# phi of the memory layers without a relu: exponential on ScalarE, clamp on GpSimd, maximum on VectorE

## The chip, the cores and the metric

The kernel runs on one core of one Trainium2 chip. The metric is the device time of one execution in microseconds (us), as the median of a few runs; lower is better. The names of the engines in the profile: PE is TensorE's matmul, PEld its weight load, ACT is ScalarE, DVE is VectorE, POOL is GpSimd, SP is SyncE, which only issues DMAs here.

## The reference

Four layers follow each other, A, B, A, B, each with a layer norm ahead of it and a residual addition behind it. The input x is 2048 x 640; there are 32 heads of 20 columns. The change concerns layer B, which splits the 2048 rows into four segments of 512:

```
phi = lambda t: jnp.where(t > 0, t + 1.0, jnp.exp(t))
for s in range(N):
    qs, ks, vs = q[:, :, s], k[:, :, s], v[:, :, s]
    logits = jnp.einsum("bhqd,bhkd->bhqk", qs, ks) * scale + mask
    p = _softmax(logits, axis=-1)
    a_dot = jnp.einsum("bhqk,bhkd->bhqd", p, vs)
    pq = phi(qs)
    num = jnp.einsum("bhld,bhde->bhle", pq, M)
    den = jnp.einsum("bhld,bhd->bhl", pq, z)[..., None] + 1e-6
    a_mem = num / den
    outs.append(g * a_mem + (1.0 - g) * a_dot)
    pk = phi(ks)
    M = M + jnp.einsum("bhld,bhle->bhde", pk, vs)
    z = z + jnp.einsum("bhld->bhd", pk)
```

So phi(q) is multiplied by a memory M that sums phi(k) v over the earlier segments, and the product is divided by phi(q) times the sum z of phi(k). A common factor of all phi(q), or of all phi(k), drops out of num / den, apart from the 1e-6. Layer A is linear attention with a similar phi, which the change leaves as it is.

## The kernel before

**Numbers.** The float32 weights are scaled by a power of two and split into an upper and a lower float16 part (`w_prep`). Two columns of 128 equal values come with each weight: `inv`, which brings a product of the scaled weight back to its true size, and `scl`, its reciprocal. A projection is three float16 matmuls per block of rows, summed in a PSUM bank in float32 (`proj_t`, L414, 128x512; `proj_n`, L429, 128x320).

**Layer B, one segment** (`b_project`): first v by `proj_n`; then, for five tiles of 128 columns, q and k by `proj_t`, in turns, each into one PSUM bank p of 128x512. `split_store` reads p twice (ScalarE L860, VectorE L861) and writes q or k in two float16 parts to DRAM, from where the attention loads them (`stacks`, L1031). Then `phi` reads p: on ScalarE an exponential with the factor `inv` (L453) and a relu with the same factor (L455); VectorE forms min(e, 1) + r (L456). phi of q is made for segments 1 to 3, phi of k for segments 0 to 2: 2 layers x 3 segments x 5 tiles x 2 = 60 calls. phi of k is turned by TensorE (L888) and multiplied with v into the memory (L898); phi of q meets the memory in `read_mem` (L482), which also divides (L489 to L492).

**Softmax attention** runs beside the projections and the layers' other work, by heads of four: scores of queries for the row maxima (`row_max`, L1045; VectorE takes the maximum with the mask, L1051), scores of keys with the maxima taken off (L1086), an exponential per bank on ScalarE (L1090), the causal cut of the diagonal block on GpSimd (L1097), and the product with v (`weigh`, L1113).

**Order.** Two generators, the layers' dense work and the attention, are woven by an estimated cost of TensorE; that order is fixed for TensorE (`MANUAL`). On the other engines a scheduler sets the order by what is ready in its model. The eight PSUM banks come from one pool (`bank`), and the allocator picks for each new tile a bank that its model sees free; TensorE's first matmul into it waits until the last reader of the tile before is done. The SBUF tiles of phi come from a pool named "er" with three buffers, which `phi_a` of layer A and `normalize` also use.

The functions and lines that the change touches: `w_prep` (the clamp L266), `scales` (L319 to L321), `phi` (L449 to L456), `read_mem` (L489) and the two calls in `b_project` (L914 and L928). GpSimd's instructions, of which there are more now, stand in one queue with the cuts L1097, the additions L506 and L1137 and the products L786.

Of the kernel before, what the change touches and what calls it, by code (L numbers as in the profile page):

```python
# [9 lines left out]
F32 = mybir.dt.float32  # L10
# [3 lines left out]
AF = mybir.ActivationFunctionType  # L14
OP = mybir.AluOpType
# [5 lines left out]
S, D, H, DH = 2048, 640, 32, 20  # L21
P = 128
# [20 lines left out]
HB = H // 2  # L43
# [101 lines left out]
class Kernel:  # L145
# [88 lines left out]
    def w_prep(self, key, stage, w, wait=0, behind=None):  # L234


        nc, cp = self.nc, self.cp
# [6 lines left out]
        with self.tc.issue_after(behind.ins) if behind else nullcontext():  # L244
            for c in range(C):
# [16 lines left out]
        inv = cp.tile([P, 1], F32, name="inv_%s%s" % key)  # L262
        scl = cp.tile([P, 1], F32, name="scl_%s%s" % key)
        nc.vector.tensor_scalar(inv.bitcast(I32), pb[:, :1].bitcast(I32), 0x7F800000, None,
                                op0=OP.bitwise_and)
        nc.vector.tensor_scalar(inv, inv, 2.0 ** -14, 2.0 ** -114, op0=OP.mult, op1=OP.max)  # L266
        self.last = nc.vector.reciprocal(scl, inv)
        self.inv[key], self.scl[key] = inv, scl
        yield 100.0
        for cols in (slice(0, HN), slice(HN, D)) if key == ("A", "k") else (slice(0, D),):  # L270
            for c in range(C):
                nc.scalar.activation(w[:, c, 0, cols], st[:, c, cols], AF.Copy, scale=scl)
                if key == ("B", "o"):
                    continue
                self.last = nc.vector.scalar_tensor_tensor(w[:, c, 1, cols], st[:, c, cols], scl, w[:, c, 0, cols],
                                                           op0=OP.mult, op1=OP.subtract)
# [31 lines left out]
    def scales(self, L):  # L308
        nc, cp = self.nc, self.cp
        io = cp.tile([P, 1], F32, name="io" + L)  # L310
        nc.vector.tensor_tensor(io, self.inv[L, "v"], self.inv[L, "o"], op=OP.mult)
        nc.vector.tensor_scalar(io, io, 1 / V_SHIFT, None, op0=OP.mult)
        self.io[L] = io
        if L == "A":
            self.io["G"] = cp.tile([P, 1], F32, name="ioG")
            nc.vector.tensor_scalar(self.io["G"], io, 1 / (P_ONE * W_SHIFT), None, op0=OP.mult)
        if L == "B":
            self.lsc = cp.tile([P, 1], F32, name="lsc")
            nc.vector.tensor_tensor(self.lsc, self.inv["B", "q"], self.inv["B", "k"], op=OP.mult)  # L319
            nc.vector.tensor_scalar(self.lsc, self.lsc, DH ** -0.5 / QK_SHIFT / QK_SHIFT, None,  # L320
                                    op0=OP.mult)  # L321

    def key_scale(self):

# [121 lines left out]
        nc.vector.scalar_tensor_tensor(e, e, 1.0, r, op0=OP.min, op1=OP.add)  # L446
        return e

    def phi(self, p, inv, dst):  # L449
        nc, sb = self.nc, self.sb  # L450
        n = p.shape[-1]
        e = sb.tile([P, 512], F32, tag="er", name="e", bufs=3)[:, :n]
        nc.scalar.activation(e, p, AF.Exp, scale=inv)  # L453
        r = sb.tile([P, 512], F32, tag="er", name="r", bufs=3)[:, :n]
        nc.scalar.activation(r, p, AF.Relu, scale=inv)  # L455
        nc.vector.scalar_tensor_tensor(dst, e, 1.0, r, op0=OP.min, op1=OP.add)  # L456

    def v_half(self, p, v, n):
        vv = v[:, :H * E1].rearrange("p (h e) -> p h e", e=E1)
# [11 lines left out]
    def read_mem(self, pq, mem, dst):  # L471

        nc, sb = self.nc, self.sb
        cut = HB * E1
        for k in range(2):
            nd = self.bank()
            cost, first = 0, True
            for t in range(C):
                a, b = LO[t] * E1, LO[t] * E1 + WID[t]
                lo, hi = max(a, k * cut), min(b, (k + 1) * cut)  # L480
                if lo < hi:
                    nc.tensor.matmul(nd[:, lo - k * cut:hi - k * cut], pq[t],  # L482
                                     mem[:, OFF[t] + lo - a:OFF[t] + hi - a],
                                     start=first, stop=True, skip_group_check=True)
                    first = False
                    cost += 4 * (hi - lo) * COL
            nd = nd[:, :cut].rearrange("p (h e) -> p h e", e=E1)
            rc = sb.tile([P, HB], F32, tag="rc", name="rc", bufs=3)
            nc.vector.scalar_tensor_tensor(rc, nd[:, :, DH], 1e-6, self.ginv[:, k * HB:(k + 1) * HB],  # L489
                                           op0=OP.add, op1=OP.mult)  # L490
            nc.vector.reciprocal(rc, rc)
            nc.vector.tensor_tensor(dst[:, k * HN:(k + 1) * HN].rearrange("p (h e) -> p h e", e=DH),  # L492
                                    nd[:, :, :DH], rc[:, :, None].to_broadcast([P, HB, DH]),
                                    op=OP.mult)
            yield cost
# [374 lines left out]
    def b_project(self, st):  # L870

        nc, sb, bp = self.nc, self.sb, self.bp
# [36 lines left out]
        for t in range(C):  # L909
            p = yield from self.proj_t(xT, w["q"], t)  # L910
            self.split_store(p, st["qd"], t, "q")
            if s > 0:
                pq = sb.tile([P, SEG], F32, tag="pq", name="pq", bufs=PQ)
                self.phi(p, self.inv["B", "q"], pq)  # L914
                st["pq"].append(pq)
            yield self.COST_T
            st["half"] = t >= 2
            made = self.proj_t(xT, w["k"], t)
            yield next(made)
            if pkT is not None:  # L920
                yield self.take(1)
                pk = pk_turn()
                yield 440
            p = yield from made
            self.split_store(p, st["kd"], t, "k")
            if s < NSEG - 1:
                pkT = bp.tile([P, SEG], F32, tag="pkT", name="pkT", bufs=1)
                self.phi(p, self.inv["B", "k"], pkT)  # L928
            yield self.COST_T
            if pk is not None:  # L930
                give(t - 1, pk)
# [513 lines left out]
```

## Time and profile before

| what | value |
|---|---|
| median of 3 runs | 1663.18 us (1662.56 to 1665.42) |
| the profiled execution | 1665.72 us |
| its span, first to last instruction | 1664.0 us |
| mean granted TensorE clock | 0.998 |
| instructions | 37840 |
| HBM | 109.32 MB read, 77.00 MB written |

The profile is one execution. A row of a group of instructions reads: line, engine, operation, what it writes <- what it reads, shape, xcount, then busy time in us, the mean of one in ns, and the idle time of the engine just ahead of them with what ended it. A row of the timeline reads: start in us, length in us, engine, line, operation, and in brackets the idle time ahead of it and what ended that. Line numbers in these rows are those of the kernel before; in the changed kernel the lines behind L325 stand four lines further down.

### The profile page before, as it was taken

The numbers are of one execution on the slowest core, as the hardware profiler recorded it, in microseconds if no ns is written. First come the engines' busy times: TensorE is split into PE (matmuls) and PEld (weight loads), VectorE is DVE, ScalarE is ACT, GpSimd is POOL, SyncE is SP. The second block draws the span as 40 slices with busy tenths as digits, with TensorE's granted clock in tenths as the row PEclk, the third lists the DMA queues.
The fourth block names the chain that finished last, engine by engine and source line by source line (L and its number), as shares of the span: only waits on it lengthen the run. The fifth ranks groups of instructions, "written<-read, shape, count | busy, mean of one in ns | idle before, by whom it ended". The sixth has DMA issues, their size and how long they took to land.

```text
span 1664.0 us, 37840 instructions
## 1 busy us (share of the span) xinstructions
PE 1618.3 (97%) x13818; PEld 1020.6 (61%) x13818; DVE 1256.1 (75%) x4014; ACT 994.3 (60%) x1888; POOL 508.5 (31%) x1048
## 2 busy tenths in 40 slices
PE   8999999999999999999999999999989999999998
PEld 6777766554565566456557777756546546645555
DVE  7788896597887887768764456838888878878772
ACT  6667543457666656667665544433675675666773
POOL 4433232023223423343351301210232342333552
PEclk9999999999999999999999999999999999999999
DMA  6414653422312432352211303623232232323422
GB/s 224 159 71 179 225 213 119 149 93 79 119 57 88 144 102 92 116 188 67 67 46 44 108 33 127 213 99 113 72 110 93 97 112 95 107 94 110 145 89 96
DMA packets 110347, 189.33 MB, mean 114 GB/s; under 512 B 14160, under 2 KB 69840, under 8 KB 107728
## 3 DMA queue, kind: packets, MB, share of 16 engines
q1 hardware_dynamic: 97536, 141.02, 26.1%
q0 software_dynamic: 3264, 24.91, 4.1%
q10 hardware_dynamic: 9360, 20.98, 3.2%
q8 instruction: 109, 1.79, 0.5%
q14 instruction: 78, 0.64, 0.1%
HBM read 109.32 MB, written 77.00 MB: 112 GB/s over the span
## 4 chain that ended last, share of the span: by engine, by line
PE 76%; DVE 11%; ACT 7%; issue 2%; DMA 2%; POOL 1%; SPq 0%; ACTq 0%; DVEq 0%; POOLq 0%
PE ps L429 30%; PE ps L414 14%; PE ps L1113 9%; PE ps L605 4%; PE ps L1086 4%; PE ps L346 4%; PE ps L1045 3%; ACT pe L1090 3%; PE ps L482 2%; DVE ps L1051 2%; PE ps L1126 2%; DVE e L446 1%; DMA x<-in_A_x 1%; PE ps L888 1%; ACT xh L401 1%
## 5 line engine op out<-in xcount | busy, mean ns | idle before, releaser
L1051 DVE CUSTOM_DVE_ANT_0 ps<-ps,maskw 128x384 f32<-128x384 f32 (+3 forms) x1024 | 472.6, 519 | 39.5 <-PE ps L1045 36.6
L1090 ACT ACTIVATE pe<-ps,lsc 128x512 f32<-128x512 f32 x640 | 393.9, 695 | 79.7 <-PE ps L1086 62.5
L1097 POOL TENSOR_SCALAR_AFFINE_SELECT pe<-pe 128x256 f32<-128x256 f32 (+1 forms) x640 | 231.4, 367 | 390.3 <-ACT pe L1090 387.1
L429 PEld LDWEIGHTS <-xT 128*128 128x128 f16 x2880 | 279.3, 98 | 111.9 <-issue 6.6
L429 PEld LDWEIGHTS <-oT 128*128 128x128 f16 x1920 | 185.9, 98 | 82.3 <-issue 7.1
L1113 PE MATMUL ps<-pe,v 128*32 128x512 f32 (+3 forms) x2048 | 156.6, 436 | 9.9 <-ACT r L455 6.2
L429 PE MATMUL ps<-w_Bo,oT 128*128 128x320 f16 x960 | 142.8, 301 | 3.8 <-ACT oT L350 2.0
L414 PE MATMUL ps<-xT,w_Bq 128*128 128x512 f16 x600 | 142.2, 382 | 2.3 <-ACT pe L1090 2.0
L1051 DVE DVE_READ_ACCUMULATOR2_ANT mg<- 128x1 f32 x1024 | 143.8, 140 | 0.0
L414 PE MATMUL ps<-xT,w_Bk 128*128 128x512 f16 x600 | 141.5, 379 | 0.8 <-ACT pe L1090 0.8
L429 PE MATMUL ps<-wm,oT 128*128 128x320 f16 x960 | 140.9, 299 | 0.7 <-DVE mg L1051 0.3
L605 PE MATMUL ps<-pk,xs 128*128 128x321 f16 (+1 forms) x960 | 136.9, 300 | 3.1 <-DVE v L625 1.7
L429 PE MATMUL ps<-w_Bv,xT 128*128 128x320 f16 x960 | 139.7, 299 | 0.0
L429 PE MATMUL ps<-w_Ak,xT 128*128 128x320 f16 x960 | 137.5, 299 | 2.0 <-DVE xT L351 1.4
L429 PE MATMUL ps<-w_Aq,xT 128*128 128x320 f16 x960 | 137.8, 299 | 0.6 <-ACT r L445 0.6
L1086 PE MATMUL ps<-qs,ks 62*128 62x384 f16 (+3 forms) x1024 | 130.5, 299 | 3.6 <-ACT pe L1090 2.2
L1045 PE MATMUL ps<-ks,qs 60*128 60x512 f16 (+3 forms) x1024 | 116.0, 297 | 3.0 <-DVE xT L351 1.6
L605 PEld LDWEIGHTS <-xs 128*128 128x128 f16 x960 | 92.9, 97 | 41.7 <-issue 4.1
L446 DVE SCALAR_TENSOR_TENSOR e<-e,r 128x320 f32<-128x320 f32 x128 | 64.8, 507 | 58.9 <-ACT r L445 58.2
L1113 PEld LDWEIGHTS ps<-pe,v 128*32 128x32 f32 x2048 | 62.9, 109 | 67.8 <-issue 50.8
L861 DVE SCALAR_TENSOR_TENSOR nat<-ps,nat 128x512 f16<-128x512 f32 x80 | 55.1, 689 | 60.8 <-ACT nat L860 60.4
L414 PEld LDWEIGHTS <-w_Bq 128*128 128x128 f16 x600 | 57.1, 98 | 69.1 <-issue 10.9
(202 smaller groups left out, 2369.6 us busy)
## 6 DMA issues: line engine op xcount, KB each, us to landing
x<-xn ACTq DMA_DIRECT2D x48, 320.0 KB
qs<-qd SPq DMA_DIRECT2D x128, 120.0 KB
ks<-kd SPq DMA_DIRECT2D x128, 120.0 KB
xo<-x SPq DMA_DIRECT2D x48, 320.0 KB
pqi<-pqd SPq DMA_DIRECT2D x32, 320.0 KB
qd<-nat SPq DMA_DIRECT2D x40, 256.0 KB
kd<-nat SPq DMA_DIRECT2D x40, 256.0 KB
x<-in_A_x SPq DMA_DIRECT2D x16, 320.0 KB
```

Source lines behind the costliest of these rows:

```text
L346: nc.tensor.transpose(pt[:, (c - c0) * P:(c - c0 + 1) * P], src[:, c * P:(c + 1) * P], self.ident)
L414: nc.tensor.matmul(p, w[:, c, a, t * P:(t + 1) * P], xT[:, c, b, :], start=k == 0, stop=k == 3 * C - 1)
L429: nc.tensor.matmul(p, xT[:, c, a, i * P:(i + 1) * P], w[:, c, b, n * HN:(n + 1) * HN], start=k == 0, stop=k == 3 * C - 1)
L446: nc.vector.scalar_tensor_tensor(e, e, 1.0, r, op0=OP.min, op1=OP.add)
L605: nc.tensor.matmul(p, xs[:, i, a, c * P:(c + 1) * P], pk[i][:, b, cols], start=i == 0 and a == b, stop=i == NT - 1 and a == 1)
L861: nc.vector.scalar_tensor_tensor(nat[:, 1], p, QK_SHIFT, nat[:, 0], op0=OP.mult, op1=OP.subtract)
L1045: nc.tensor.matmul(bs[par][:, a:a + n], qs[r, p, i * P:(i + 1) * P], ks[r, p, :n], start=True, stop=True)
L1051: nc.vector.tensor_tensor_reduce(bs[par][:, a:a + n], bs[par][:, a:a + n], self.maskw[:, SEG - n:], 1.0, NEG, OP.add, OP.max, G["mg"][:, p ...
L1086: nc.tensor.matmul(b[:, a:a + n], ks[r, p, j * P:(j + 1) * P], qs[r, p, j * P:], start=True, stop=True)
L1090: nc.scalar.activation(e, b, AF.Exp, scale=self.lsc)
L1097: self.select = nc.gpsimd.affine_select(d, d, pattern=pat, compare_op=OP.is_ge, fill=0.0, base=0, channel_multiplier=-1)
L1113: nc.tensor.matmul(G["pv"][32 * h4:32 * h4 + 32, j * P:], v[j][:, h * E1:h * E1 + 32], G.pop((p, par, j)), start=j == 0, stop=j == 2, skip ...
```

## The change

phi no longer brings p to its true size. ScalarE still takes the exponential of p times `inv`. GpSimd then takes, in place, the minimum of it and 1 and multiplies by `scl`. VectorE adds the larger of p and 0, read from PSUM. The result is phi times `scl`, in the units of p; since all of phi(q) and all of phi(k) carry one factor each, the quotient is the same, and the 1e-6 of the denominator is multiplied by both factors (`eps_B`). The bound of `inv` is raised to 2^-30 for the q and k weights of layer B.

```diff
-        nc.vector.tensor_scalar(inv, inv, 2.0 ** -14, 2.0 ** -114, op0=OP.mult, op1=OP.max)
+        nc.vector.tensor_scalar(inv, inv, 2.0 ** -14, 2.0 ** (-30 if key in (("B", "q"), ("B", "k")) else -114),
+                                op0=OP.mult, op1=OP.max)
...
+            self.eps = cp.tile([P, 1], F32, name="eps_B")
+            nc.vector.scalar_tensor_tensor(self.eps, self.scl["B", "q"], 1e-6, self.scl["B", "k"],
+                                           op0=OP.mult, op1=OP.mult)
...
-    def phi(self, p, inv, dst):
+    def phi(self, p, key, dst):
         nc, sb = self.nc, self.sb
-        n = p.shape[-1]
-        e = sb.tile([P, 512], F32, tag="er", name="e", bufs=3)[:, :n]
-        nc.scalar.activation(e, p, AF.Exp, scale=inv)
-        r = sb.tile([P, 512], F32, tag="er", name="r", bufs=3)[:, :n]
-        nc.scalar.activation(r, p, AF.Relu, scale=inv)
-        nc.vector.scalar_tensor_tensor(dst, e, 1.0, r, op0=OP.min, op1=OP.add)
+        e = sb.tile([P, 512], F32, tag="er", name="e", bufs=3)
+        nc.scalar.activation(e, p, AF.Exp, scale=self.inv[key])
+        nc.gpsimd.tensor_scalar(e, e, 1.0, self.scl[key], op0=OP.min, op1=OP.mult)
+        nc.vector.scalar_tensor_tensor(dst, p, 0.0, e, op0=OP.max, op1=OP.add)
...
-            nc.vector.scalar_tensor_tensor(rc, nd[:, :, DH], 1e-6, self.ginv[:, k * HB:(k + 1) * HB],
+            nc.vector.scalar_tensor_tensor(rc, nd[:, :, DH], self.eps, self.ginv[:, k * HB:(k + 1) * HB],
...
-                self.phi(p, self.inv["B", "q"], pq)
+                self.phi(p, ("B", "q"), pq)
...
-                self.phi(p, self.inv["B", "k"], pkT)
+                self.phi(p, ("B", "k"), pkT)
```

TensorE's order is the same, instruction by instruction. What moves on the others, at three places of the first layer B, second segment. ScalarE, around the third tile's k and q (e and r are phi's, pe the attention's exponential, nat the split for DRAM); before:

```order
L453 ACTIVATE e<-ps,inv_Bk 128x512
L455 ACTIVATE r<-ps,inv_Bk 128x512
L1090 ACTIVATE pe<-ps,lsc 128x512 x4
L860 ACTIVATE nat<-ps 128x512
L453 ACTIVATE e<-ps,inv_Bq 128x512
L455 ACTIVATE r<-ps,inv_Bq 128x512
L1090 ACTIVATE pe<-ps,lsc 128x512 x2
L1071 ACTIVATE mt<-pm 32x128
```

and now:

```order
L458 ACTIVATE e<-ps,inv_Bk 128x512
L1094 ACTIVATE pe<-ps,lsc 128x512 x4
L864 ACTIVATE nat<-ps 128x512
L458 ACTIVATE e<-ps,inv_Bq 128x512
L1094 ACTIVATE pe<-ps,lsc 128x512 x2
L1075 ACTIVATE mt<-pm 32x128
```

The exponentials of the attention stand directly behind phi's; nothing else moved here. On GpSimd, where before there were only cuts (pe) and the products of layer A (pqi), the new step stands among them, at and behind the same place:

```order
L459 TENSOR_SCALAR e<-e,scl_Bq 128x512
L1101 AFFINE_SELECT pe<-pe 128x2x128 x2
L1101 AFFINE_SELECT pe<-pe 128x128
L459 TENSOR_SCALAR e<-e,scl_Bk 128x512
L1101 AFFINE_SELECT pe<-pe 128x128 x3
L1101 AFFINE_SELECT pe<-pe 128x2x128 x4
L459 TENSOR_SCALAR e<-e,scl_Bq 128x512
L1101 AFFINE_SELECT pe<-pe 128x2x128 x2
L790 TENSOR_TENSOR pqi<-pqi,rca 128x640 x3
```

Each new step stands ahead of the cuts whose exponentials follow phi's on ScalarE. On VectorE phi's step mostly keeps its place; here, three tiles on, it passes a row maximum (mask). Before:

```order
L784 RECIPROCAL rca<-rca 128x32
L1051 ISA ps,mg<-ps,maskw 128x512
L1051 ISA mg 128x1
L456 SCALAR_TENSOR_TENSOR pq<-e,r 128x512
L1051 ISA ps,mg<-ps,maskw 128x512
```

and now:

```order
L788 RECIPROCAL rca<-rca 128x32
L460 SCALAR_TENSOR_TENSOR pq<-ps,e 128x512
L1055 ISA ps,mg<-ps,maskw 128x512
L1055 ISA mg 128x1
L1055 ISA ps,mg<-ps,maskw 128x512
```

The row maximum now stands behind phi's step, which waits for GpSimd. On SP, a load of keys passes the row-maximum writes (`max_rows`) at two places, and at one place three DMAs change their order.

## The prediction

> **What bounds the kernel now.** I read the page's first part, then busy time by stretch, then who waits for the lines that the change touches.
>
> ```profile
> span 1664.0 us, 37840 instructions
> PE 1618.3 (97%) x13818; PEld 1020.6 (61%) x13818; DVE 1256.1 (75%) x4014; ACT 994.3 (60%) x1888; POOL 508.5 (31%) x1048
> ```
>
> TensorE (PE) is busy for 97% of the span, so an edit elsewhere pays only through the 46 us in which PE stands idle, and costs only if it makes new waits there. The sum is made against the profiled execution: 1665.72 us, of which the span is 1664.0 and 1.7 lies around it. It is 0.15% above the median of the runs (1663.18), so I carry the difference over to the median.
>
> phi of layers B runs 60 times: 30 for q (three segments of five tiles, two layers) and 30 for k. These rows give busy time over eight stretches that hold all sixty (two of them shown, and the sum):
>
> ```profile
> 375.00:452.00 77.00, 72.37 (x694) 38.41 (x692) 61.16 (x220) 54.11 (x97) 23.45 (x53) 1.00 0.31 100
> 515.00:600.00 85.00, 83.70 (x748) 47.41 (x746) 67.31 (x221) 54.23 (x99) 31.66 (x57) 1.00 0.39 127
> sum 526.00, PE 507.96 PEld 265.04 DVE 376.34 ACT 336.79 POOL 151.47; mean PE 63.49 PEld 33.13 DVE 47.04 ACT 42.10 POOL 18.93
> ```
>
> After the window and its length come PE, PEld, DVE, ACT and POOL. PE idles for 526.0 - 508.0 = 18 us here; that is all that can be won at sight. ScalarE (ACT) works 64% of the time, VectorE (DVE) 72%, GpSimd (POOL) 29%. Next, who waits for the relu on L455:
>
> ```profile
>   DVE pq L456: 16.9, 14
>   DVE pkT L456: 16.1, 16
>   PE ps L1113: 6.2, 7
>   ACT nat L860: 4.7, 8
> ```
>
> The third row matters: seven times PE waits 6.2 us in all for a relu. One of the seven, in order of time:
>
> ```profile
> 395.27 0.69 ACT L453 ACTIVATE e<-ps,inv_Bq 128x512 f32<-128x512 f32 x1 [0.76 <-DVE nat L861]
> 395.85 0.68 ACT L455 ACTIVATE r<-ps,inv_Bq 128x512 f32<-128x512 f32 x1
> 396.42 1.27 ACT L1090 ACTIVATE pe<-ps,lsc 128x512 f32<-128x512 f32 x2
> 396.56 0.69 DVE L456 SCALAR_TENSOR_TENSOR pq<-e,r 128x512 f32<-128x512 f32 x1 [1.33 <-ACT r L455]
> 396.68 0.64 PE L1113 MATMUL ps<-pe,v 128*32 128x512 f32 x4 [1.33 <-ACT r L455]
> ```
>
> L1113 reads nothing of the relu. It opens a new PSUM bank, and that bank was the projection's: the relu, ending at 396.53, was its last reader. So two things are at stake: ScalarE's time, and how long phi holds a bank.
>
> **The change part by part.** These rows carry the durations:
>
> ```profile
> L453 ACT ACTIVATE e<-ps,inv_Bq 128x512 f32<-128x512 f32 x30 | 20.9, 697 | 17.2 <-DVE nat L861 17.2
> L455 ACT ACTIVATE r<-ps,inv_Bq 128x512 f32<-128x512 f32 x30 | 20.8, 694 | 0.0
> L456 DVE SCALAR_TENSOR_TENSOR pq<-e,r 128x512 f32<-128x512 f32 x30 | 20.7, 690 | 17.4 <-ACT r L455 16.9
> L861 DVE SCALAR_TENSOR_TENSOR nat<-ps,nat 128x512 f16<-128x512 f32 x80 | 55.1, 689 | 60.8 <-ACT nat L860 60.4
> L1097 POOL TENSOR_SCALAR_AFFINE_SELECT pe<-pe 128x256 f32<-128x256 f32 x384 | 158.2, 415 | 199.4 <-ACT pe L1090 197.2 <-ACT oT L350 0.5 <-POOL pe L1097 0.3
> L1097 POOL TENSOR_SCALAR_AFFINE_SELECT pe<-pe 128x128 f32<-128x128 f32 x256 | 73.2, 296 | 190.9 <-ACT pe L1090 190.0
> L506 POOL TENSOR_TENSOR xn<-xn,xo 128x320 f32<-128x320 f32 x56 | 48.9, 873 | 148.3 <-ACT xn L505 145.2 <-issue 2.9
> L489 DVE SCALAR_TENSOR_TENSOR rc<-ps,gate 128x16 f32<-128x16 f32 x48 | 7.1, 151 | 0.1
> ```
>
> *The relu goes.* Neighbours on ScalarE overlap: in the five rows above, e starts at 395.27, r at 395.85 and the next exponential at 396.42, so one relu holds the queue for 0.575 us. 60 x 0.575 = 34.5 us leave ScalarE, mostly beside PE's work.
>
> *VectorE's step* now takes one input from PSUM instead of two from SBUF. L861 has that kind of input and costs 689 ns against L456's 690: no difference.
>
> *GpSimd's step*, 128x512 f32 with one tensor input, is not in the trace. The lower end is the select with one input: (415 - 296) / 128 = 0.93 ns an element, so 415 + 256 x 0.93 = 653 ns. The upper end is the addition with two inputs: 873 ns at 320 elements, 1.2 us at 512 if its start costs what the select's does (0.18 us; 0.18 + 512 x 2.17 ns = 1.29, less if more of it is start). I take 0.70, near the select, since the new step reads one tensor too. The Trainium skill (GPSIMD Engine Reference, Performance versus the Vector engine) says that ordinary elementwise arithmetic does not belong on GpSimd, and gives 769 ns for 512 elements in a tight unrolled loop; by an estimate from that, 0.77, the first term below would be 3.4 instead of 2.8 us. No run here shows the step yet.
>
> *Queue.* I looked at what stands ahead of each new step in GpSimd's order, with its end in this trace: in 55 of 60 places it is over before the exponential ends, in the other five it is 0.1 to 0.9 us late. So GpSimd starts at once nearly always.
>
> *How long the bank is held* (term 1). Before: to the relu's end, 0.575 us after the exponential's. After: hop 0.035 (396.53 to 396.56 above), GpSimd 0.70, hop 0.035, VectorE 0.69: 1.46 us after it. With the old places of the banks that would hurt: 16 of the 60 are wanted within 0.2 us of the relu's end. But the allocator knows of the longer life. By the PSUM addresses of the two built programs it hands 45 of the 60 banks to another user than before. I laid the trace's times over the new addresses: of 60, eight are wanted earlier than 1.46 us after the exponential's end. The first, one in the middle and the last:
>
> ```profile
> 320.81 0.69 ACT L453 ACTIVATE e<-ps,inv_Bk 128x512 f32<-128x512 f32 x1 [0.76 <-DVE nat L861]
> 322.51 1.66 PE L429 MATMUL ps<-wm,oT 128*128 128x320 f16 x11
> ...
> 544.29 0.69 ACT L453 ACTIVATE e<-ps,inv_Bq 128x512 f32<-128x512 f32 x1 [0.95 <-DVE nat L861]
> 546.03 1.24 PE L414 MATMUL ps<-xT,w_Bk 128*128 128x512 f16 x5
> ...
> 1378.26 0.69 ACT L453 ACTIVATE e<-ps,inv_Bq 128x512 f32<-128x512 f32 x1 [0.82 <-DVE nat L861]
> 1380.34 0.66 PE L888 MATMUL ps<-ident,pkT 128*128 128x128 f32 x4 [0.40 <-ACT pe L1090]
> ```
>
> At the first, e ends at 321.50, the bank is free at 322.96, and PE wants it at 322.51: 0.45 late, 0.49 with the 0.05 us from a release to PE. The eight give 2 x 0.49, 2 x 0.34, 2 x 0.46, 2 x 0.11 = **+2.8 us**. With GpSimd at 1.2 us the same reading finds 30 banks short, 12.2 us in all; at 0.60, 2.0.
>
> *What the freed time wins* (term 2). At the seven L1113 places the new bank's last reader is the exponential that followed the relu; at 396.68 it ended at 397.11, and without the relu ends 0.575 earlier, at 396.54. So PE starts at 396.59 instead of 396.68: what is late next is ScalarE again, 0.1 us behind. 7 x 0.1 = 0.7. Two transposes wait behind a run of exponentials that starts at a relu's end:
>
> ```profile
> 421.10 0.44 PE L346 MATMUL ps<-ident,pqi 128*128 128x128 f32 x2 [0.53 <-ACT pe L1090]
> ```
>
> 0.5 each, 1.0. Nine further releases by a relu leave 0.05 to 0.1 each, 0.7 together. Sum **-2.4 us**.
>
> *Banks that swap where no relu stands ahead* (term 3). In this row PE starts a matmul whose bank, by the new addresses, is freed by an exponential only at 742.90:
>
> ```profile
> 742.21 2.42 ACT L1090 ACTIVATE pe<-ps,lsc 128x512 f32<-128x512 f32 x4 [1.06 <-PE ps L1086]
> 742.23 0.38 PE L1086 MATMUL ps<-qs,ks 62*128 62x512 f16 x1
> 742.95 0.37 PE L1086 MATMUL ps<-qs,ks 62*128 62x512 f16 x1 [0.34 <-ACT pe L1090]
> ```
>
> PE already waits for that exponential one matmul later, so the first matmul (0.21 us to the next one) is what moves behind the wait. Six such places (734, 742, 747, 1348, 1380, 1523) at 0.25: **+1.5 us**.
>
> *VectorE's wait* (term 4). Before, its step could start 0.61 after the exponential's end, now 0.77; row maxima queue behind it in order. The first two rows of who waits for L455 give 30 places in which VectorE stood waiting; 30 x 0.16 = 4.8 us of VectorE, which is 72% busy, so most is caught up. I let a tenth reach PE: **+0.5 us**; the bounds are 0 and, at 1.2 us of GpSimd, 30 x 0.66 = 20 us, a fifth of it 4.
>
> *The port between VectorE and GpSimd.*
>
> ```profile
> 422.71 0.82 DVE L778 TENSOR_TENSOR pqi<-pqi,z 128x640 f32<-128x640 f32 x1
> 422.84 0.96 POOL L1097 TENSOR_SCALAR_AFFINE_SELECT pe<-pe 128x256 f32<-128x256 f32 x1 [0.17 <-ACT pe L1090]
> ...
> 426.60 0.69 DVE L456 SCALAR_TENSOR_TENSOR pq<-e,r 128x512 f32<-128x512 f32 x1
> 426.70 0.85 POOL L1097 TENSOR_SCALAR_AFFINE_SELECT pe<-pe 128x256 f32<-128x256 f32 x1 [2.90 <-ACT pe L1090]
> ```
>
> Two selects of 0.41 us take 0.96 and 0.85 while VectorE reads two SBUF tensors. The old L456 did that; the new one reads one. I count no gain, as the select is not what PE waits for there, and no loss, as L778 covers little of a stretch. The Trainium skill (SBUF — State Buffer, Who interferes with whom) says that a VectorE instruction with two SBUF inputs holds off a GpSimd instruction that reads SBUF; the trace agrees, and the new step may itself be held off behind L778.
>
> *The rest.* eps_B is one more VectorE instruction of one column in the opening, and L489 takes its 1e-6 from a column instead of an immediate: 151 ns x 48 stay. The other clamp changes a constant. Two loads of keys pass the row-maximum writes on SP's queue, 0.4 us of issue each. Nothing.
>
> Sum: 2.8 - 2.4 + 1.5 + 0.5 = **+2.4 us**. 1663.18 + 2.4 = 1665.6 us; in the profiled execution, 1668.1.
>
> **The rivals.** A measurement of this kernel can tell about 0.2% (3.3 us) from no change.
>
> *Faster.* ScalarE is late more often than the rows of PE's idle time show, because a matmul's modelled end hides stalls of up to 0.2 us. If each of the 16 places where PE starts within 0.2 us of a relu's end wins 0.45 of the 0.575, that is -7.2; with the banks never late, terms 1 and 3 fall away: 1656 us. For it: 6.2 us of waits name the relu. Against: the next release is again ScalarE's, 0.1 us behind.
>
> *Slower.* GpSimd takes 1.2 us. It decides from about 0.8: then a bank is held 1.56 us, term 1 is 3.8 and the sum +3.6. At 1.2 it is 12.2, term 4 is 4, and 12.2 - 2.4 + 1.5 + 4 = +15: 1678 us; half way, 1670. For it: all additions on GpSimd cost that much. Against: they read two tensors.
>
> *Nothing reaches PE.* All four terms drown in PE's 97%: 1663.2.
>
> **How the numbers follow.** Forecast 0.40 and nothing reaches PE 0.10, nearly all within 0.2%; slower 0.33; faster 0.17. The forecast itself is 1665.6. Low 1658 keeps most of the faster case, high 1676 most of the slower. Faster by over 0.2%: 0.17; within: 0.49; slower: 0.34.
>
> **What would show it.** In the profile after: ACT's busy time down by about 41 us (60 x 0.694), no L455 of ScalarE; GpSimd's new group x60 at 0.65 to 0.75 us; VectorE's step at 0.69 with idle time before it put down to GpSimd; PE's waits naming the VectorE step of phi in some eight places, 0.1 to 0.5 us each; PE's waits at L1113 shorter, now naming L1090. The prediction is wrong if GpSimd's mean is over 0.8 us, if PE's idle time in the eight stretches leaves 16 to 22 us, or if a wait grows in the attention stretches without phi.

## The result and the profile after

| | before | after |
|---|---|---|
| median | 1663.64 us (1662.56 to 1665.42, 4 runs) | 1724.87 us (1724.13 to 1726.67, 4 runs) |
| ratio | | 1.0366, 95% interval 1.0354 to 1.0379 |

The change makes the kernel 61 us slower, far above the forecast of 1665.6 and above the range's upper end of 1676. The first part of the page of after:

```profile
span 1722.4 us, 37846 instructions
PE 1632.8 (95%) x13818; PEld 1017.9 (59%) x13818; DVE 1261.3 (73%) x4015; ACT 967.5 (56%) x1828; POOL 621.8 (36%) x1108
```

ScalarE has 27 us less to do, GpSimd 113 us more, VectorE the same as before. TensorE executes the same matmuls in the same order, so the two traces can be laid over each other matmul by matmul. The eight stretches of the prediction, cut at the same matmuls in the trace of after (two of them, and the sum):

```profile
376.60:465.30 88.70, 76.17 (x693) 38.40 (x691) 61.31 (x218) 50.09 (x87) 41.46 (x62) 0.98 0.27 87
528.30:625.70 97.40, 86.69 (x747) 47.54 (x746) 67.70 (x221) 48.66 (x89) 50.12 (x67) 0.98 0.35 112
sum 586.00, PE 524.07 PEld 264.25 DVE 379.35 ACT 308.48 POOL 263.75; mean PE 65.51 PEld 33.03 DVE 47.42 ACT 38.56 POOL 32.97
```

The same work takes 586.0 us where it took 526.0: the whole loss of 60 us lies in the stretches with phi. TensorE's idle time in them grows from 18 to 586.0 - 524.1 = 62 us. The other 16 us of the loss are in its busy time. A part of that is the granted clock: it is 0.98 in four of these eight stretches (both shown rows), and 0.98 in one of the eight before; 0.02 of some 90 us in three more stretches is about 5 us, an estimate. The remainder may be short stalls that a matmul's modelled end hides; that is not shown. VectorE works as much as before, in 60 us more. So nothing got more work that was short of time; something waits. The groups of phi in after (the new lines: L459 is GpSimd's step, L460 VectorE's):

```profile
L459 POOL TENSOR_SCALAR e<-e,scl_Bq 128x512 f32<-128x512 f32 x30 | 60.0, 2000 | 64.2 <-ACT e L458 63.6 <-ACT mt L1075 0.6
L459 POOL TENSOR_SCALAR e<-e,scl_Bk 128x512 f32<-128x512 f32 x30 | 59.9, 1995 | 68.4 <-ACT e L458 68.3
L460 DVE SCALAR_TENSOR_TENSOR pq<-ps,e 128x512 f32<-128x512 f32 x30 | 20.7, 692 | 62.4 <-POOL e L459 62.4
L460 DVE SCALAR_TENSOR_TENSOR pkT<-ps,e 128x512 f32<-128x512 f32 x30 | 20.8, 692 | 60.1 <-POOL e L459 60.1
```

GpSimd's step takes 2.0 us, not 0.70. VectorE's own step costs what was said (692 ns), but VectorE stands idle ahead of it for 122.5 us, where it stood 33.0 us for the relu. Who waits on TensorE, in the view of the waits:

```profile
PE ps L1117 <- DVE pq L460: 7.9, 5, 2.0
PE pm L1073 <- DVE pq L460: 6.8, 7, 1.1
PE ps L418 <- DVE pq L460: 3.8, 2, 2.0
PE ps L1049 <- DVE pkT L460: 3.7, 4, 1.0
```

Eleven such rows name L460, with 39.4 us in 34 places; I had foreseen eight places of 0.1 to 0.5 us. One place in order of time, first in after:

```profile
415.38 0.69 DVE L865 SCALAR_TENSOR_TENSOR nat<-ps,nat 128x512 f16<-128x512 f32 x1 [0.30 <-ACT nat L864]
416.11 0.69 ACT L458 ACTIVATE e<-ps,inv_Bq 128x512 f32<-128x512 f32 x1 [0.76 <-DVE nat L865]
416.77 0.60 PE L1049 MATMUL ps<-ks,qs 60*128 60x512 f16 x6
416.90 2.00 POOL L459 TENSOR_SCALAR e<-e,scl_Bq 128x512 f32<-128x512 f32 x1 [2.06 <-ACT e L458]
418.93 0.69 DVE L460 SCALAR_TENSOR_TENSOR pq<-ps,e 128x512 f32<-128x512 f32 x1 [2.85 <-POOL e L459]
419.54 0.69 DVE L1055 CUSTOM_DVE_ANT_0 ps<-ps,maskw 128x512 f32<-128x512 f32 x1
419.67 0.22 PE L1073 MATMUL pm<-ident,m 128*32 128x128 f16 x1 [0.74 <-DVE pq L460]
```

and the same place in before:

```profile
408.51 0.69 DVE L861 SCALAR_TENSOR_TENSOR nat<-ps,nat 128x512 f16<-128x512 f32 x1 [0.60 <-ACT nat L860]
409.25 0.60 PE L1045 MATMUL ps<-ks,qs 60*128 60x512 f16 x6
410.53 0.69 DVE L456 SCALAR_TENSOR_TENSOR pq<-e,r 128x512 f32<-128x512 f32 x1 [1.33 <-ACT r L455]
411.14 0.69 DVE L1051 CUSTOM_DVE_ANT_0 ps<-ps,maskw 128x512 f32<-128x512 f32 x1
411.50 0.22 PE L1069 MATMUL pm<-ident,m 128*32 128x128 f16 x1
```

GpSimd starts 0.1 us after the exponential, nearly as foreseen (0.035), and hands over in 0.03; the hops don't explain the loss. But TensorE has filled banks with scores for the row maxima (L1049, at 416.77), and the first of these maxima starts on VectorE 2.8 us later, behind L460, where it took 1.9 us before. Counted from the split (L865, L861), the transposition L1073 starts 4.29 us later instead of 2.99.

Two things happen at once in such a place: phi's bank is held until VectorE's step ends (2.82 us from the exponential's end in the median of the 60, and 0.58 us before, to the relu's end), and VectorE stands in line with the row maxima behind it. The waits name L460 for both. Which of the two it is, the trace doesn't tell.

### The profile page after: what moved, and what is told of

Same layout as the page of the kernel before. It is cut to its first block, busy times and chain, and to the rows that moved or that the text cites. A ratio compares the mean times of both kernels' runs of the same rounds, so it can differ in the third digit from the quotient of the medians.

```text
span 1722.4 us, 37846 instructions
## 1 busy us (share of the span) xinstructions
PE 1632.8 (95%) x13818; PEld 1017.9 (59%) x13818; DVE 1261.3 (73%) x4015; ACT 967.5 (56%) x1828; POOL 621.8 (36%) x1108
## 4 chain that ended last, share of the span: by engine, by line
PE 66%; DVE 16%; POOL 7%; ACT 6%; issue 3%; DMA 1%; SPq 0%; ACTq 0%; DVEq 0%; POOLq 0%
PE ps L433 31%; PE ps L418 8%; PE ps L1117 7%; POOL e L459 6%; PE ps L609 5%; PE ps L1090 4%; DVE ps L1055 4%; PE ps L350 4%; PE ps L1049 3%; ACT pe L1094 2%; PE ps L486 2%; ACT e L458 2%; PE ps L1130 1%; DVE nat L865 1%; DVE pq L460 1%
## 5 line engine op out<-in xcount | busy, mean ns | idle before, releaser
L1101 POOL TENSOR_SCALAR_AFFINE_SELECT pe<-pe 128x256 f32<-128x256 f32 (+1 forms) x640 | 227.2, 365 | 296.7 <-ACT pe L1094 294.6
L433 PEld LDWEIGHTS <-oT 128*128 128x128 f16 x1920 | 185.3, 98 | 84.9 <-issue 10.8
L1117 PE MATMUL ps<-pe,v 128*32 128x512 f32 (+3 forms) x2048 | 162.5, 445 | 19.0 <-ACT pe L1094 8.2
L1090 PE MATMUL ps<-qs,ks 62*128 62x384 f16 (+3 forms) x1024 | 134.2, 300 | 9.7 <-ACT pe L1094 3.5
L1049 PE MATMUL ps<-ks,qs 60*128 60x512 f16 (+3 forms) x1024 | 120.2, 297 | 9.1 <-DVE pkT L460 3.7
L418 PEld LDWEIGHTS <-w_Bk 128*128 128x128 f16 x600 | 57.9, 98 | 73.3 <-issue 13.2
L354 ACT ACTIVATE oT<-ps 128x384 f16<-128x384 f32 (+1 forms) x128 | 55.6, 443 | 78.5 <-PE ps L350 72.7
```

The source lines that it names most:

```text
L418: nc.tensor.matmul(p, w[:, c, a, t * P:(t + 1) * P], xT[:, c, b, :], start=k == 0, stop=k == 3 * C - 1)
L433: nc.tensor.matmul(p, xT[:, c, a, i * P:(i + 1) * P], w[:, c, b, n * HN:(n + 1) * HN], start=k == 0, stop=k == 3 * C - 1)
L1049: nc.tensor.matmul(bs[par][:, a:a + n], qs[r, p, i * P:(i + 1) * P], ks[r, p, :n], start=True, stop=True)
L1090: nc.tensor.matmul(b[:, a:a + n], ks[r, p, j * P:(j + 1) * P], qs[r, p, j * P:], start=True, stop=True)
L1101: self.select = nc.gpsimd.affine_select(d, d, pattern=pat, compare_op=OP.is_ge, fill=0.0, base=0, channel_multiplier=-1)
L1117: nc.tensor.matmul(G["pv"][32 * h4:32 * h4 + 32, j * P:], v[j][:, h * E1:h * E1 + 32], G.pop((p, par, j)), start=j == 0, stop=j == 2, skip ...
```

## The experiments

The theory I started from was the prediction's term 1 at its true price: the bank. Laid over the new addresses as in the prediction, a hold of 2.76 us leaves 35 of the 60 banks short, 38 us in all. The rivals: VectorE's place in line (term 4); GpSimd's queue, which is fuller by 113 us; and VectorE reading PSUM, or the new places of the banks, whatever GpSimd costs.

**price.** A program of its own with GpSimd's step in several forms, each six times:

```diff
+    for _ in range(R):
+        pool.tensor_scalar(f, e, 1.0, scl, op0=OP.min, op1=OP.mult)
+    for _ in range(R):
+        pool.tensor_scalar(f, e, 1.0, 0.5, op0=OP.min, op1=OP.mult)
+    for _ in range(R):
+        pool.tensor_scalar(f, e, 1.0, None, op0=OP.min)
+    for _ in range(R):
+        pool.tensor_scalar(f, e, 0.5, None, op0=OP.mult)
...
+    for _ in range(R):
+        pool.tensor_scalar(f, e, 0.5, 1.0, op0=OP.mult, op1=OP.add)
```

> A program without the layers: GpSimd alone runs each form of instruction six times on 128x512 f32, then VectorE alone, then GpSimd beside VectorE. Its output is only ones, so its time as a whole says nothing. Main theory: the step costs 2.0 us by itself, 1.95 to 2.05 us with VectorE idle; if the cost is per element, 256 columns take about 1.0 and 128 about 0.6 us. Rival A, it is held off by VectorE in the kernel: alone it takes 0.7 to 0.9 us, and 2.0 only beside VectorE's two-input additions. Rival B, it is the column operand or the second operation: then the forms with one immediate take 0.7 to 1.0 us, and only those with a column or two operations 2.0. The cut over 512 columns should take 0.65 us, from 415 and 296 ns at 256 and 128.

The groups, in this order: the change's form (L39), the same with immediates (L43), minimum alone (L45), factor alone (L47, by a column L49), factor and sum (L51), addition of two tensors (L53), copy (L57), the change's form on 256 and 128 columns (L59, L61), a cut (L63); then VectorE's clamp alone (L68) and its addition of two tensors (L72), and both beside each other (L76 with L78):

```profile
L39 POOL TENSOR_SCALAR e<-e,scl 128x512 f32<-128x512 f32 x6 | 12.0, 1992 | 5.6 <-DVE scl L36 5.1
L43 POOL TENSOR_SCALAR f<-e 128x512 f32<-128x512 f32 x6 | 11.5, 1917 | 0.5
L45 POOL TENSOR_SCALAR f<-e 128x512 f32<-128x512 f32 x6 | 8.9, 1484 | 0.5
L47 POOL TENSOR_SCALAR f<-e 128x512 f32<-128x512 f32 x6 | 8.9, 1489 | 0.5
L49 POOL TENSOR_SCALAR f<-e,scl 128x512 f32<-128x512 f32 x6 | 9.4, 1560 | 0.6
L51 POOL TENSOR_SCALAR f<-e 128x512 f32<-128x512 f32 x6 | 3.7, 617 | 0.5
L53 POOL TENSOR_TENSOR f<-e,g 128x512 f32<-128x512 f32 x6 | 7.6, 1262 | 0.5
L57 POOL COPY f<-e 128x512 f32<-128x512 f32 x6 | 3.7, 612 | 0.4
L59 POOL TENSOR_SCALAR f<-e,scl 128x256 f32<-128x256 f32 x6 | 6.8, 1140 | 0.6
L61 POOL TENSOR_SCALAR f<-e,scl 128x128 f32<-128x128 f32 x6 | 4.3, 712 | 0.6
L63 POOL TENSOR_SCALAR_AFFINE_SELECT f<-e 128x512 f32<-128x512 f32 x6 | 3.7, 612 | 0.4
L68 DVE TENSOR_SCALAR h<-b,scl 128x512 f32<-128x512 f32 x6 | 2.9, 486 | 0.2
L72 DVE TENSOR_TENSOR h<-b,d 128x512 f32<-128x512 f32 x6 | 4.2, 692 | 0.2
L76 POOL TENSOR_SCALAR g<-h,scl 128x512 f32<-128x512 f32 x6 | 14.6, 2435 | 17.6 <-DVE h L74 17.1
L78 DVE TENSOR_TENSOR f<-b,d 128x512 f32<-128x512 f32 x18 | 14.7, 814 | 0.6
```

The step costs 1.99 us with VectorE idle, so it isn't VectorE that makes it slow: rival A is gone. It isn't the column (1917 without it) nor the second operation alone (one operation takes 1484 already): rival B holds only in part. What is cheap is a kind of operation: the cut, the copy, and the pair of factor and sum take 612 to 617 ns; a minimum or a factor alone takes 1.48 us, with one tensor input. So the number of inputs, by which I chose the nearest row, doesn't set the price. From 256 and 512 columns the form costs (1992 - 1140) / 256 = 3.33 ns a column and 0.29 us of start; 256 and 128 columns cost 1.14 and 0.71 us, a little over the 1.0 and 0.6 expected.

**clamp_on_dve.**

```diff
-        nc.gpsimd.tensor_scalar(e, e, 1.0, self.scl[key], op0=OP.min, op1=OP.mult)
+        nc.vector.tensor_scalar(e, e, 1.0, self.scl[key], op0=OP.min, op1=OP.mult)
```

> The changed kernel with the clamp on VectorE in place of GpSimd; all else as in the change, the exponential in true size, the maximum read from PSUM. Main theory (the 2.0 us of GpSimd are the loss): the bank is held about 1.1 to 1.4 us after the exponential, VectorE gets 60 x 0.4 to 0.7 = 24 to 42 us more work; the time returns to 1662 to 1670 us. Rival (the new places of the banks, or VectorE reading p from PSUM, are the loss): it stays above 1690 us.

1665.34 us, ratio 1.0004 (0.9994 to 1.0013): as before the change, although VectorE reads p from PSUM, the banks are handed out for a longer life, and VectorE works 31 us more (510 and 534 ns for each clamp). So the loss hangs on GpSimd standing between the exponential and VectorE. The run is a sum of gains and losses (ScalarE is relieved here too), so it doesn't price the parts.

**early_max.** The bank taken out of the chain:

```diff
-        nc.gpsimd.tensor_scalar(e, e, 1.0, self.scl[key], op0=OP.min, op1=OP.mult)
-        nc.vector.scalar_tensor_tensor(dst, p, 0.0, e, op0=OP.max, op1=OP.add)
+        nc.vector.tensor_scalar(dst, p, 0.0, None, op0=OP.max)
+        nc.gpsimd.tensor_scalar(e, e, 1.0, self.scl[key], op0=OP.min, op1=OP.mult)
+        nc.vector.tensor_tensor(dst, dst, e, op=OP.add)
```

> The changed kernel with the maximum of p and 0 taken from PSUM by an instruction of VectorE of its own that waits for nothing of phi, and VectorE's sum of it and GpSimd's result behind it. So the bank is free after the exponential, and GpSimd's 2.0 us stand only between the exponential and the sum. If the loss is the bank held for GpSimd: the 35 us of new starts of PE that wait for phi's step only because of a bank go, 1685 to 1695 us. If the loss is VectorE standing in order behind GpSimd: VectorE still waits 50 to 60 times, and the time stays above 1710 us.

1719.03 us, ratio 1.0329 (1.0313 to 1.0344). The bank is now free 0.72 us after the exponential in the median, and 54 of the 61 us stay: the bank alone can't be the loss. VectorE waits less for GpSimd than in the change, but only because its own maximum fills part of the wait:

```profile
L460 DVE TENSOR_TENSOR pq<-pq,e 128x512 f32<-128x512 f32 x30 | 25.2, 839 | 30.0 <-POOL e L459 30.0
L460 DVE TENSOR_TENSOR pkT<-pkT,e 128x512 f32<-128x512 f32 x30 | 23.5, 785 | 33.3 <-POOL e L459 33.3
```

It still comes to the row maxima only when GpSimd is done. Its sums take 785 to 839 ns, and it has 42 us more work, so this run alone isn't a price of the standing.

**pool_idle_work** and **wait_only**, both on the kernel before, with its relu: the first gives GpSimd the work and lets nobody wait for it, the second puts it in VectorE's way and leaves the bank as it was.

```diff
         nc.vector.scalar_tensor_tensor(dst, e, 1.0, r, op0=OP.min, op1=OP.add)
+        nc.gpsimd.tensor_scalar(sb.tile([P, 512], F16, tag="jk", name="jk", bufs=1), e, 1.0, inv, op0=OP.min, op1=OP.mult)
```

> The kernel before, with relu and all, and on GpSimd one more instruction of 2.0 us per phi (minimum and factor of the exponential, written to a tile of its own that nobody reads). So GpSimd's queue is as full as in the changed kernel, its cuts and products stand behind these instructions, but nobody waits for them. If the loss comes through GpSimd's queue (the cuts late, and with them the products with v): 1680 to 1700 us. If it comes by VectorE's wait or by the bank: 1663 to 1668 us.

1670.37 us, ratio 1.0037 (1.0023 to 1.0051): 6 us, not 16 to 36, though 2 us above the lower range. GpSimd's fuller queue costs little; some of the 6 us may be VectorE's step, which reads two tensors of SBUF here and takes 760 to 775 ns beside GpSimd instead of 690.

```diff
         nc.scalar.activation(r, p, AF.Relu, scale=inv)
+        nc.gpsimd.tensor_scalar(e, e, 1.0, 1.0, op0=OP.min, op1=OP.mult)
         nc.vector.scalar_tensor_tensor(dst, e, 1.0, r, op0=OP.min, op1=OP.add)
```

> The kernel before with relu on ScalarE, so that the bank is free at the relu's end as before; between the exponential and VectorE's step GpSimd takes the minimum with 1 in place (1.92 us by the price run). Only VectorE waits longer, in order, by about 1.92 + 0.07 - 0.61 = 1.4 us; no bank is held longer. If VectorE's place in line is the loss: 1705 to 1720 us. If it is the bank: 1664 to 1672 us.

1715.69 us, ratio 1.0309 (1.0293 to 1.0324). The bank is freed by the relu as ever, and 51 us of loss are there. VectorE's step waits 113.2 us for GpSimd:

```profile
L456 DVE SCALAR_TENSOR_TENSOR pq<-e,r 128x512 f32<-128x512 f32 x30 | 26.1, 870 | 56.1 <-POOL e L455 56.1
L456 DVE SCALAR_TENSOR_TENSOR pkT<-e,r 128x512 f32<-128x512 f32 x30 | 24.6, 820 | 57.1 <-POOL e L455 57.1
```

The step also takes 820 to 870 ns beside GpSimd, and GpSimd's queue is fuller; by pool_idle_work these two are worth some 6 us or a little more, an estimate. The waits of TensorE in this run:

```profile
PE ps L1086 <- DVE mg L1051: 13.3, 19, 1.5
PE ps L1113 <- ACT r L454: 6.6, 7, 2.1
PE ps L888 <- DVE pkT L456: 3.9, 2, 2.3
PE ps L1045 <- DVE mg L1051: 3.8, 5, 1.4
```

The largest names the row maxima now, and phi's own step has 3.9 us. The same stall of VectorE shows under the name of whatever VectorE finishes first behind it for TensorE.

**late_add** and **behind_maxima** keep the instructions and move VectorE's step out of the way: phi hands it back as a function (lq for q, lk for k) and the caller issues it later. The lines for q in late_add:

```diff
             self.split_store(p, st["kd"], t, "k")
+            if lq:
+                with self.tc.issue_after(self.nat.ins):
+                    lq()
```

> The run with the early maximum again, but VectorE's sum of the maximum and GpSimd's result is put behind the split of the next projection in VectorE's order, some 4 to 8 us later, so that GpSimd is done when its turn comes. GpSimd works as long as before, VectorE as much as in that run, but doesn't stand. If VectorE's standing is the loss: 1664 to 1674 us. If GpSimd's queue, or the two-input sums of VectorE against GpSimd, are the loss: above 1695 us.

1686.36 us, ratio 1.0135 (1.012 to 1.015): 33 us better than early_max with the same instructions in another order, but 12 us above the upper end of what was expected. VectorE waits 5.2 us for GpSimd in all. New waits take the place: the sum for k now comes too late for its transposition (first row), and a product of layer A comes late from GpSimd (second row). What makes up the rest of the 22 us over the kernel before is not shown.

```profile
PE ps L891 <- DVE pkT L460: 5.2, 10, 1.2
PE ps L350 <- POOL pqi L790: 4.1, 2, 2.9
```

In behind_maxima the change's own step moves, with the bank:

```diff
             yield next(made)
+            if s > 0:
+                with self.tc.issue_after(self.lastmax.ins) if self.lastmax is not seen else nullcontext():
+                    lq()
```

> The changed kernel, same instructions, but VectorE's step of phi is put behind the row maxima that come next in the program: eight of them for q, four for k, where the attention has any there. VectorE then works on maxima while GpSimd clamps, and the bank of phi is held longer than in the changed kernel, by up to 8 x 0.5 us less the 2.0 it stood. If VectorE's standing in line is the loss: 1680 to 1700 us, less than 70 us of waits for GpSimd on VectorE. If the held bank is the loss: 1725 us or more.

1694.09 us, ratio 1.0173 (1.0157 to 1.0188). The bank is held longer than in the change (4.0 us in the mean, 2.9 there), and half of the loss is gone. VectorE's idle time for GpSimd falls from 122.5 to 75.6 us (under 70 was expected):

```profile
L459 DVE SCALAR_TENSOR_TENSOR pkT<-ps,e 128x512 f32<-128x512 f32 x30 | 20.7, 691 | 52.0 <-POOL e L458 52.0
L459 DVE SCALAR_TENSOR_TENSOR pq<-ps,e 128x512 f32<-128x512 f32 x30 | 20.6, 687 | 23.6 <-POOL e L458 23.6
```

**stand_no_bank** and **bank_no_stand** were made to take each of the two alone. In the first the step reads the exponential twice, so the maximum is left out; the second, further down, has no relu and no GpSimd step, and a late reader of one column of p, issued behind the row maxima as in behind_maxima. The first:

```diff
-        nc.vector.scalar_tensor_tensor(dst, p, 0.0, e, op0=OP.max, op1=OP.add)
+        nc.vector.scalar_tensor_tensor(dst, e, 0.0, e, op0=OP.max, op1=OP.add)
```

> The changed kernel, but VectorE's step takes the exponential twice and not p, so that the maximum is left out and the bank is free at the exponential's end. GpSimd's 2.0 us stay, VectorE stands in line as in the changed kernel, ScalarE has no relu. If the prediction's term 1 is right at the true price (laid over the new addresses, a bank held 2.76 us leaves 35 banks short, 38 us in all): 1683 to 1692 us. If VectorE's standing alone makes the loss: 1714 to 1726 us.

1723.15 us, ratio 1.0352 (1.0334 to 1.0369): the loss of the change without its bank. The step takes 820 to 853 ns here beside GpSimd, 0.14 us more than in the change, which by the slope below is worth some 6 us; so the bank's share in the change is some 2 to 8 us, an estimate; the intervals of the two runs alone are 2 to 3 us to either side. The waits name what stands behind VectorE's step:

```profile
PE ps L1090 <- DVE mg L1055: 11.9, 18, 1.8
PE ps L350 <- DVE mg L1055: 5.3, 6, 1.3
```

The second:

```diff
+        nc.vector.scalar_tensor_tensor(dst, e, 1.0, e, op0=OP.min, op1=OP.add)
+        return lambda: nc.vector.tensor_copy(sb.tile([P, 1], F32, tag="jk", name="jk", bufs=2), p[:, :1])
```

> The run without a relu, and one more instruction of VectorE that reads one column of p and keeps it, behind the row maxima that come next (eight for q, four for k), so that phi's bank is held some 2 to 5 us after the exponential while VectorE and GpSimd do what they did without it. If held banks cost what term 1 says (38 us at 2.76 us): 1685 to 1700 us. If it is VectorE's standing that costs: 1655 to 1665 us.

1664.84 us, ratio 1.0008 (0.9998 to 1.0017), at the end of what standing foresaw and 20 us under the least that term 1 foresaw. The hold is 2.6 us in the mean, but 1.3 in the median, as the places without maxima release at once. Something else, too, keeps this run from settling what held banks cost. The allocator knows of the late reader and hands out the banks accordingly: the reading of term 1, redone with this program's addresses and this trace's holds, finds two late banks, 0.2 us in all, not 38. The trace agrees. Those who waited for the late reader are two groups of weight loads, 1.1 us together, and no matmul:

```profile
  PEld L1095: 0.8, 2
  PEld L433: 0.3, 2
```

So the run shows that a longer hold is cheap where the allocator has counted on it. It doesn't show what a bank costs that comes late without VectorE standing; no run does.

**pool_128_columns, pool_272_columns, pool_400_columns** vary the length of GpSimd's step; the columns left out keep the bare exponential. The edit of the first (the others have 272 and 400 in place of 128):

```diff
-        nc.gpsimd.tensor_scalar(e, e, 1.0, self.scl[key], op0=OP.min, op1=OP.mult)
+        nc.gpsimd.tensor_scalar(e[:, :128], e[:, :128], 1.0, self.scl[key], op0=OP.min, op1=OP.mult)
```

> The changed kernel with GpSimd's step on the first 128 of 512 columns only (the other columns keep the bare exponential): 0.71 us by the price run, which is what the prediction took for the whole step. If the prediction's sum was right but for the price: 1663 to 1668 us (it said 1665.6). If VectorE's wait goes to PE in proportion, 58 us for 1.46 us more per phi, 0.17 us more here give 7 us: 1668 to 1673 us.

> The changed kernel with GpSimd's step on 272 of 512 columns only: 0.285 + 272 x 0.00333 = 1.19 us by the price run, the upper end of the prediction, which said 1678 us for it. If VectorE's wait goes to PE in proportion from 0.71 us (1671.1) to 1.99 us (1724.9), 42 us per us: 1691 us. Between 1674 and 1682 the prediction's sum holds at its upper end.

> The same on 400 of 512 columns: 1.62 us. In proportion 1709 us. If the loss sets in only from a certain length on (VectorE has slack of about 1 us in each place), it is steeper here than between 128 and 272 columns.

| GpSimd's step | VectorE idle for it | time | ratio, interval |
|---|---|---|---|
| 0.72 us | 63.0 us | 1671.08 us | 1.0042 (1.0027 to 1.0057) |
| 1.20 us | 82.5 us | 1689.40 us | 1.0146 (1.0132 to 1.016) |
| 1.62 us | 105.3 us | 1707.33 us | 1.0252 (1.0238 to 1.0266) |
| 2.00 us | 122.5 us | 1724.87 us | 1.0366 (1.0354 to 1.0379) |

Nearly a straight line: from the first to the last row (1724.9 - 1671.1) / (2.00 - 0.72) = 42 us for each microsecond of GpSimd's step, and from row to row 38, 43 and 46. Sixty calls would make 60 us of it, so seven tenths reach the end; of the time that VectorE stands more, 122.5 - 63.0 = 59.5 us, it is nine tenths. Between 0.72 and 2.00 us there is no length that is free. One reservation: the length isn't all that differs. Between a tile's split and phi's step VectorE executes 137, 165, 174 and 182 instructions in the four traces, all sixty places together (193 in before), since the scheduler orders VectorE anew for each program; and the bank is held as long as the step is. The three runs came out as the proportional reading foresaw (1668 to 1673, 1691, 1709), and the first not as the prediction's sum at its own price. Already in the first VectorE waits for GpSimd in 58 of 60 places; the rows give the time in all, how often, and the longest:

```profile
DVE pq L460 <- POOL e L459: 34.3, 28, 2.1
DVE pkT L460 <- POOL e L459: 28.7, 30, 1.6
```

**relu_on_dve** and **no_relu** ask what the relief of ScalarE is worth.

```diff
-        nc.scalar.activation(r, p, AF.Relu, scale=inv)
+        nc.vector.tensor_scalar(r, p, 0.0, inv, op0=OP.max, op1=OP.mult)
```

> The kernel before with the relu made by VectorE (maximum with 0 times the factor, from PSUM) in place of ScalarE, no GpSimd. ScalarE loses 60 x 0.575 = 34 us, VectorE gains 60 x 0.69 = 41 us, and the bank is free at the exponential's end. If ScalarE's relief is worth what I reckoned as term 2, 1661 to 1664 us; if the faster rival was right about it, 1655 to 1658; if VectorE at near 80% in these stretches becomes late, 1667 to 1675.

1666.1 us, ratio 1.0008 (0.9998 to 1.0018), in none of the three ranges: what the relief wins (next run) is gone again with 42 us more work on VectorE.

```diff
-        r = sb.tile([P, 512], F32, tag="er", name="r", bufs=3)[:, :n]
-        nc.scalar.activation(r, p, AF.Relu, scale=inv)
-        nc.vector.scalar_tensor_tensor(dst, e, 1.0, r, op0=OP.min, op1=OP.add)
+        nc.vector.scalar_tensor_tensor(dst, e, 1.0, e, op0=OP.min, op1=OP.add)
```

> The kernel before without the relu, which is left out altogether: VectorE's step adds the exponential in its place, from SBUF. So ScalarE is relieved of 60 x 0.575 us, the bank is free at the exponential's end, and nothing is added anywhere: the most that the idea of the change could win. By term 2 of the prediction 1661 to 1663 us (2.4 us less than before); by the faster rival 1656 to 1658 us.

1654.9 us, ratio 0.994 (0.9927 to 0.9952): 10.0 us less than before, four times term 2 and more than the faster rival. So there was something to win. No form that computes the whole of phi got it: the clamp and the relu on VectorE give it back there, and GpSimd's cheapest forms in the price run, 0.61 us, would by the line above still give 1671.1 - 0.11 x 38 = 1667 us (an estimate, which carries the slope of 38 us per us between the first two rows of the table a little further down).

## Why the prediction was wrong

**GpSimd's price.** The step "I take 0.70, near the select, since the new step reads one tensor too" failed. It takes 1.99 us alone and 2.00 in the kernel. The upper end of 1.29, from the addition of two tensors, was no bound either: the addition does cost 1.26 us at 512 columns, as worked out, but the minimum with a factor costs more than any row of the trace had shown. The figure of 769 ns that I quoted from the Trainium skill (GPSIMD Engine Reference, Performance versus the Vector engine) is for a tight loop; the cut, the copy and the pair of factor and sum are even under it (612 to 617 ns), and the clamp takes 2.6 times as long. That page's rule, that elementwise work belongs on VectorE, is the one that the runs bear out: clamp_on_dve is 60 us faster than the change.

**VectorE's wait (term 4).** The second failure, and the one that would have been left at the right price, has two parts. The first is "30 x 0.16 = 4.8 us of VectorE": the thirty places are those in which VectorE stood waiting for the relu, and the others were left out. At the price that I took (0.72 us) VectorE waits in 58 places and for 63.0 us, 30.0 more than the 33.0 for the relu. The second is "I let a tenth reach PE". Up to 0.72 us it is about four tenths (against no_relu, 16 us of time for 63.0 - 22.7 = 40 us more of standing), and from there to 2.00 us nine tenths. VectorE at 72% looked as if it could catch up, but the share of busy time says nothing of what stands directly behind the waiting instruction: the row maxima, whose banks and results TensorE waits for in wait_only and stand_no_bank. Even at the price that I took, the time is 1671.1 us, not 1665.6; at 1.2 us it is 1689.4, where the slower rival said 1678. That rival had the right sign and the right condition (a price over 0.8 us), but not the path: 12.2 of its 15 us were the bank's, and it let a fifth of VectorE's wait reach TensorE.

**The bank (term 1).** At the true hold the same reading of addresses and times gives 38 us; with VectorE standing anyway the bank adds some 2 to 8 us (the change against stand_no_bank). What late banks would cost by themselves is open, since in bank_no_stand they hardly come late. A reason for the small share may be that the method counts each late bank as if the next one were still wanted at its old time; once TensorE has waited for one thing, what follows is late as well, and its banks are free by then. That is argued, not tried.

**ScalarE's relief (term 2).** Said -2.4; with the relu left out and nothing put in its place the runs give -10.0. That is more than ScalarE's relief: in no_relu the bank is also free 0.58 us earlier, and VectorE waits 22.7 us ahead of its step where it waited 33.0. The faster rival looked for the missing part in stalls that a matmul's modelled end hides. In the profiles most of it is plain idle time: the span of no_relu is 10.8 us shorter than that of before (1653.2), TensorE's busy time only 3.5 us (1614.8). So the reading of single rows of waits missed more than the hidden stalls did. ACT's busy time in the change fell by 26.8 us, not 41: neighbours on ScalarE overlap, and overlapping time counts once.

**What held.** GpSimd starts at once (0.1 us after the exponential in 54 of 60 places); the hops are 0.03 to 0.1 us; VectorE's step is the same from PSUM (692 ns); eps_B and the loads on SP don't show. Term 3, the swapped banks, was not tried by itself; clamp_on_dve has new places of the banks too and comes out as before the change, but among gains and losses that cancel, so it bounds the term only loosely. Two signs of being wrong that the prediction had named are there in the profile of after: GpSimd's mean over 0.8 us, and TensorE's idle time outside 16 to 22 us.

The sum that the runs give: relief -10, VectorE standing and GpSimd's work +68 on top of it (stand_no_bank against no_relu, some 6 us of it the slower step), the bank the rest of the 61 us.

## What to carry to other kernels

An operation that no trace shows has no nearest row by its operands; measure it alone before it goes into a chain, GpSimd's above all. An engine that waits in order costs what stands behind it, not what its mean load suggests: look at the next instructions in its queue and who waits for them. And where a wait names an instruction, ask whether the wait is for its data, its bank, or only for its engine to go on; an order that lets other work past it, and a run without the bank's reader, tell these apart. When a run is meant to hold a bank late, look first whether anybody wants that bank: an allocator that knows of the hold gives it to a later user.

## What the runs showed of the hardware

- GpSimd's price depends on the kind of operation: on 128x512 f32 with one tensor input 0.61 to 0.62 us (cut, copy, factor and sum), 1.48 (a minimum or a factor alone), 1.56 (a factor by a column), 1.92 to 1.99 (minimum and factor).
- VectorE's addition of two SBUF tensors and GpSimd's clamp slow each other: 692 to 814 ns in the mean and 1992 to 2435 ns in the price run. The single durations of that addition (lowest, median, highest) in the view of its line:

```profile
L78 DVE TENSOR_TENSOR f<-b,d x18: 681/693/1061, 141.5 to 156.0; 128x512 f32<-128x512 f32 x18
```

Twelve of the eighteen go at full speed, six take 0.37 us longer, one beside each clamp, and a clamp takes 0.44 us more. With one input from PSUM VectorE isn't slowed in the same place of the kernel: its step takes 692 ns in after, and 820 to 853 in stand_no_bank, where it reads SBUF alone. The Trainium skill (SBUF — State Buffer, Who interferes with whom) says that a VectorE instruction with two SBUF inputs contends with a GpSimd instruction that reads SBUF, which this run shows too. The section calls the shared pair of ports an exclusive lock; a lock for the length of a whole clamp this run doesn't show, since three additions pass beside one clamp.
